# Mixture of experts on one core: the four pieces of the next expert's rows are requested in one slot, first in that slot

## Chip, cores and metric

One core of a Trainium2 chip runs the whole program. Five engines work beside each other and meet through semaphores: TensorE (PE, with its weight loads shown as PEld), VectorE (DVE), ScalarE (ACT), GpSimd (POOL) and SyncE (SP). In the part of the program that matters here, SP issues nearly all transfers, one after another. The metric is the device time of one execution in microseconds (us); lower is better.

## What is computed

Three stages follow each other: a gated linear attention, a mixture of eight experts of which each token takes one, and a dense feed-forward layer with `h * cos(h)`. The change touches the second stage:

```
for e in range(E):                       # E = 8, D = 384, F = 1024
    mask = e_idx == e
    h = np.maximum(x[mask] @ w1[e], 0.0)
    ye = h @ w2[e]
    out[mask] = gate_w[mask, None] * eom[mask, e, None] * ye
```

## The kernel before

The attention stage leaves the scaled rows of all tokens in DRAM, sorted by expert: `xs` holds 448 places (`CAP`) for each expert, a row being 384 values and the token's number (385 words). The expert stage runs from about 222 us to 505 us of the profile; the feed-forward stage after it fills the rest.

**Slots.** The expert stage is a loop over 66 slots `s` (line 314): eight slots for each expert, `s = 8e + m`, and two at the end. In slot `s` the PE multiplies one 128-wide slice of the hidden layer of expert `e` (`mm1`, nine products of 128x448, lines 622 to 625), then the second product of the slice two slots back (`mm2`, nine products, lines 201 to 203). Every product is written as three, with high and low parts of both factors: after `mm1`, ACT writes the high part `hi` (line 189) and DVE the low part `lo` (line 190). Behind these two, the list `ev[s]` of the slot is worked off in the order in which `at(s, ...)` filled it. Every engine takes its own instructions in program order, and an instruction that waits holds up all that stand behind it on its engine.

**What the list of a slot holds** (lines 283 to 307), in this order before the change:

- 24 conversions of a weight block from 64-bit numbers to 32-bit ones, for the later stage. `conv_load` issues the block (`cs`, 512 KB) three slots ahead; `conv_a` (ACT line 227, DVE lines 228 to 232) and one slot later `conv_b` (DVE lines 238 to 241) work on it; `conv_store` (line 245) writes it back.
- `W.split`: ACT rounds two quarters of an expert weight tile (`wh<-ws`, line 113), POOL subtracts for one of them and DVE for the other (`wl<-ws,wh`, line 117). `W.load` (`ws`, 384 KB, line 100) then reloads a staging buffer, four halves ahead. Its issue on SP waits until both subtractions are done.
- `trans_x(e+1, d)` in slots `8e+4`, `8e+5`, `8e+6`, for d = 0, 1, 2: the PE transposes one third of the next expert's rows, piece by piece (four transposes, line 169, one for each of the four pieces of 112 rows), into one PSUM bank. The bank has no second buffer. ACT (`yh`, line 614) and DVE (`yl`, line 615) then split it, and the transposes of the next d wait for that.
- `ids(e+1)` in slot `8e+7`: POOL copies the token numbers out of the row buffer `xe` (`id`, line 178), and SP writes them to a table in DRAM (`idtab`, line 179).
- `load_x(e+2, r)` for the pieces r = 0 to 3 (`xe<-xs`, 168 KB each, line 162), one piece in each of the slots `8e+7`, `8e+8`, `8e+9` and `8e+10`.

**What ties them.** The row buffer `xe` has one copy, so the first piece for expert e+2 can be requested only when the last transposes of expert e+1 (slot `8e+6`) and the copy of its token numbers are done. The first four transposes that read these rows stand at the end of slot `8e+12`. The rows of expert 1 are loaded ahead of the loop, all four pieces together (line 273). So six gathers, of the experts 2 to 7, lie inside the loop. "The turn to expert 3" below means the transposes in slots 20 to 22, and so on for the others.

Of the kernel before, what the change touches and what calls it, by code (L numbers as in the profile page):

```python
# [18 lines left out]
NT, DM, E, F, FF = 3072, 384, 8, 1024, 2048  # L19
# [9 lines left out]
NR = CAP // RT  # L29
# [17 lines left out]
def build(tc, A, O):  # L47
    nc = tc.nc
    sp = nc.sync
    with ExitStack() as top:  # L50
        const = top.enter_context(tc.tile_pool(name="const", bufs=1))
        dram = top.enter_context(tc.tile_pool(name="dram", bufs=1, space=DRAM))
        xs = dram.tile([XROWS, XW], F32, name="xs")
        idtab = dram.tile([NT + CAP, 1], I32, name="idtab")
        wffn = dram.tile([8, 128, PW], F32, name="wffn")

        ident = const.tile([128, 128], F32, name="ident")
        ones = const.tile([128, 128], BF16, name="ones")
        zeros = const.tile([128, 128], BF16, name="zeros")
        ctab = const.tile([128, E, GMAX], F32, name="ctab")  # L60
        acc = const.tile([128, E], BF16, name="acc")
        plast = const.tile([128, NU, NP], F32, name="plast")
        flag = const.tile([128, 1], I32, name="flag")

        with tc.manual_schedule(), ExitStack() as rows:
            c = dict(locals())
            c["W"] = W = Weights(tc, A, c, top)
            c["ya"] = top.enter_context(tc.tile_pool(name="ya", bufs=1, side="right"))
            c["xa"] = rows.enter_context(tc.tile_pool(name="xa", bufs=1, side="right"))
            attention(tc, A, c)  # L70
            W.more(top)
            moe_ffn(tc, A, O, c)
        general(tc, A, O, c)
# [50 lines left out]
def moe_ffn(tc, A, O, c):  # L124
# [8 lines left out]
    with ExitStack() as ctx:  # L133
# [15 lines left out]
        with ExitStack() as mctx:  # L149
# [130 lines left out]
            def at(s, fn, *a):  # L280
                ev.setdefault(s, []).append((fn, a))

            for i in range(24):
                t = 6 + 23 * i // 10
                at(t - 3, conv_load, i)
                at(t, conv_a, i)
                at(t + 1, conv_b, i)
                at(t + 1, conv_store, i)
# [12 lines left out]
            for e in range(E - 1):  # L301
                for d in range(KD):
                    at(8 * e + 4 + d, trans_x, e + 1, d)
                at(8 * e + 7, ids, e + 1)
                for r in range(NR):
                    if e + 2 < E:
                        at(8 * e + 7 + r, load_x, e + 2, r)


            for d in range(KD):  # L310
# [893 lines left out]
```

## Time and profile before

| | before |
|---|---|
| median of three runs | 926.71 us (918.55, 926.71, 928.77) |
| time of the profiled execution | 921.53 us |
| its span, first to last instruction | 919.7 us |
| PE busy | 832.2 us (90%) |
| DVE busy | 733.6 us (80%) |
| ACT busy, POOL busy | 386.8 us, 413.7 us |

The profile shows one execution. The time beside the span (1.8 us) lies before the first and after the last instruction. A timeline row gives start, duration, engine, line, operation and names; a bracket at its end gives how long the engine stood idle before it and what released it. A PE that is busy need not be at full speed: the granted clock of a stretch is 1.00 at 2.4 GHz and 0.50 at 1.2 GHz, and a mean between them says that both occurred. Matmuls are pipelined, so the durations of neighbouring rows overlap; pace is read from their starts.

### The profile page before, as it was taken

Reading aid. Unit: us, or ns where it says so; the run is one execution under the profiler, and the core shown is the slowest. Engines: PE = TensorE matmul, PEld = TensorE weight load, DVE = VectorE, ACT = ScalarE, POOL = GpSimd, SP = SyncE. Lnnn points to the kernel's source line nnn. Section 1 sums busy time; section 2 is a strip of 40 time slices with the busy share of each in tenths; the row PEclk is TensorE's granted clock in tenths of the full one; section 3 lists DMA queues with packets and bytes.
Section 4 is the critical chain, followed back from the end, with each engine's and each line's share of the span. In section 5 each row is a group of like instructions: output and inputs, shape, how many; then the busy total and the mean of one; then the engine's idle time right before and its main releaser. Section 6 shows DMA issues by size and latency. Waiting matters only on the chain.

```text
span 919.7 us, 14462 instructions
## 1 busy us (share of the span) xinstructions
PE 832.2 (90%) x5253; PEld 740.9 (81%) x5253; DVE 733.6 (80%) x1288; ACT 386.8 (42%) x740; POOL 413.7 (45%) x369
## 2 busy tenths in 40 slices
PE   6887677789899898898899999999999999999995
PEld 5766566677788797797799898989999999999885
DVE  6999999886797796886876887778777777787990
ACT  3674566435343343353344444333333333333440
POOL 3546575643122222221225476544644554545652
PEclk7898899798899898999989999999999999999998
DMA  9995646203675855955846200000000000000001
GB/s 185 294 308 155 172 122 174 96 28 99 163 177 174 213 130 192 222 131 199 215 145 145 36 18 1 32 4 1 35 1 0 35 1 1 35 1 1 35 1 38
DMA packets 42033, 92.26 MB, mean 100 GB/s; under 512 B 12576, under 2 KB 19872, under 8 KB 41952
## 3 DMA queue, kind: packets, MB, share of 16 engines
q1 hardware_dynamic: 38880, 81.79, 34.0%
q0 software_dynamic: 3072, 9.45, 2.8%
q8 instruction: 43, 0.70, 0.3%
q14 instruction: 38, 0.31, 0.1%
HBM read 69.93 MB, written 21.29 MB: 99 GB/s over the span
## 4 chain that ended last, share of the span: by engine, by line
PE 58%; DVE 25%; DMA 9%; issue 4%; ACT 1%; POOL 1%; SPq 1%; DVEq 0%; POOLq 0%; ACTq 0%
PE ps L622 9%; PE ps L623 9%; PE ps L625 9%; PE o L374 6%; PE o L372 6%; PE o L373 6%; DMA xe<-xs 5%; DVE r L705 4%; PE o L201 3%; PE o L202 3%; PE o L203 3%; DVE S_sb L816 3%; DVE sc L754 2%; DVE a L738 2%; DVE d L731 2%
## 5 line engine op out<-in xcount | busy, mean ns | idle before, releaser
L368 POOL TENSOR_TENSOR lo<-r,hi 128x512 fp32r<-128x512 f32 (+1 forms) x96 | 148.1, 1543 | 172.4 <-ACT hi L367 91.5
L117 POOL TENSOR_TENSOR wl<-ws,wh 128x384 fp32r<-128x384 f32 x96 | 101.3, 1055 | 220.7 <-ACT wh L113 164.8
L622 PE MATMUL ps<-yh,wh 128*128 128x512 f32 (+1 forms) x480 | 189.2, 394 | 0.2 <-ACT yh L614 0.2
L623 PE MATMUL ps<-yh,wl 128*128 128x512 f32 (+1 forms) x480 | 187.3, 390 | 0.0
L625 PE MATMUL ps<-yl,wh 128*128 128x512 f32 (+1 forms) x480 | 135.0, 390 | 0.0
L367 ACT CAST hi<-r 128x512 fp32r<-128x512 f32 (+1 forms) x96 | 56.2, 586 | 168.7 <-DVE r L362 167.8
L630 DVE TENSOR_SCALAR n<-ps 128x512 f32<-128x512 f32 x96 | 66.2, 690 | 68.6 <-PE ps L625 68.6
L374 PE MATMUL o<-wh,lo 128*128 128x384 f32 x352 | 119.0, 338 | 1.3 <-POOL lo L368 1.3
L372 PE MATMUL o<-wl,hi 128*128 128x384 f32 x352 | 118.6, 337 | 0.0
L373 PE MATMUL o<-wh,hi 128*128 128x384 f32 x352 | 118.3, 336 | 0.0
L625 PEld LDWEIGHTS ps<-yl,wh 128*128 128x128 f32 x480 | 92.9, 194 | 16.1
L622 PEld LDWEIGHTS ps<-yh,wh 128*128 128x128 f32 x480 | 93.1, 194 | 11.8 <-ACT yh L614 0.3
L623 PEld LDWEIGHTS ps<-yh,wl 128*128 128x128 f32 x480 | 92.7, 193 | 11.3
L638 ACT ACTIVATE r<-r,quarter 128x512 f32<-128x512 f32 x96 | 69.6, 724 | 73.8 <-DVE r L637 73.8
L189 ACT ACTIVATE hi<-ps 128x448 fp32r<-128x448 f32 x64 | 34.9, 545 | 101.5 <-PE ps L625 98.9
L113 ACT CAST wh<-ws 128x384 fp32r<-128x384 f32 x160 | 74.8, 508 | 4.5 <-DMA ws<-in_wmoe 4.5
L637 DVE SCALAR_TENSOR_TENSOR r<-n,r 128x512 f32<-128x512 f32 x96 | 70.1, 730 | 3.3
L201 PE MATMUL o<-hi,wh 128*128 128x448 f32 x192 | 71.9, 374 | 0.0
L202 PE MATMUL o<-hi,wl 128*128 128x448 f32 x192 | 71.5, 373 | 0.0
L203 PE MATMUL o<-lo,wh 128*128 128x448 f32 x192 | 71.2, 371 | 0.0
L373 PEld LDWEIGHTS o<-wh,hi 128*128 128x128 f32 x352 | 66.1, 188 | 4.3
L372 PEld LDWEIGHTS o<-wl,hi 128*128 128x128 f32 x352 | 66.2, 188 | 3.9
(152 smaller groups left out, 1582.2 us busy)
## 6 DMA issues: line engine op xcount, KB each, us to landing
ws<-in_wmoe SPq DMA_DIRECT2D x64, 384.0 KB, 5.9
qkf<-in_qkf SPq DMA_DIRECT2D x46, 288.0 KB, 6.4
cs<-in_wffn SPq DMA_DIRECT2D x24, 512.0 KB, 6.9
wffn<-ca SPq DMA_DIRECT2D x24, 256.0 KB, 5.2
ws<-wffn SPq DMA_DIRECT2D x16, 384.0 KB, 3.9
xs<-xe SPq DMA_DIRECT2D x7, 770.0 KB, 10.2
v<-in_v SPq DMA_DIRECT2D x24, 200.0 KB, 4.8
xe<-xs SPq DMA_DIRECT2D x28, 168.4 KB, 8.4
```

The costliest lines, as they stand in the source:

```text
L113: self.nc.scalar.copy(out=h, in_=w)
L117: (eng or self.nc.gpsimd).tensor_tensor(out=l, in0=w, in1=h.bitcast(F32), op=ALU.subtract)
L201: pe.matmul(yps[e][d], wh[:, cs], hi, start=m == 0, stop=False)
L202: pe.matmul(yps[e][d], wl[:, cs], hi, start=False, stop=False)
L203: pe.matmul(yps[e][d], wh[:, cs], lo, start=False, stop=m == FT - 1)
L368: pool.tensor_tensor(out=los, in0=r[:, cs], in1=his.bitcast(F32), op=ALU.subtract)
L372: pe.matmul(o, hi, wl[:, cs], start=m == 0, stop=False)
L373: pe.matmul(o, hi, wh[:, cs], start=False, stop=False)
L374: pe.matmul(o, lo, wh[:, cs], start=False, stop=m == NF - 1)
L622: nc.tensor.matmul(out, wh[:, ws[d]], xh[:, d, :], start=d == 0, stop=False)
L623: nc.tensor.matmul(out, wl[:, ws[d]], xh[:, d, :], start=False, stop=False)
L625: nc.tensor.matmul(out, wh[:, ws[d]], xl[:, d, :], start=False, stop=d == 2)
```

## The change

The entries for `ids` and `load_x` are put into the slots' lists first, ahead of the conversions and the weight loads, and all four pieces go into slot `8e+7`. Nothing else differs: the same instructions, buffers and sizes.

```
@@ -280,6 +280,12 @@
             def at(s, fn, *a):
                 ev.setdefault(s, []).append((fn, a))
 
+
+            for e in range(E - 1):
+                at(8 * e + 7, ids, e + 1)
+                for r in range(NR):
+                    if e + 2 < E:
+                        at(8 * e + 7, load_x, e + 2, r)
             for i in range(24):
@@ -301,10 +307,6 @@
             for e in range(E - 1):
                 for d in range(KD):
                     at(8 * e + 4 + d, trans_x, e + 1, d)
-                at(8 * e + 7, ids, e + 1)
-                for r in range(NR):
-                    if e + 2 < E:
-                        at(8 * e + 7 + r, load_x, e + 2, r)
```

SP's queue around slot 15, where the rows of expert 3 are requested, before. The row with x2 holds the weight loads of slots 14 and 15:

```order
L220 DMA cs<-in_wffn 128x512
L100 DMA ws<-in_wmoe 128x768 x2
L173 TENSOR_LOAD start
L179 REGISTER_ALU
L179 DMA idtab<-id 112x4x1
L162 DMA xe<-xs 112x385
L245 DMA wffn<-ca 128x512
L220 DMA cs<-in_wffn 128x512
L100 DMA ws<-in_wmoe 128x768
L162 DMA xe<-xs 112x385
L100 DMA ws<-in_wmoe 128x768
L162 DMA xe<-xs 112x385
```

The same place of the queue in the changed kernel:

```order
L220 DMA cs<-in_wffn 128x512
L100 DMA ws<-in_wmoe 128x768
L173 TENSOR_LOAD start
L179 REGISTER_ALU
L179 DMA idtab<-id 112x4x1
L162 DMA xe<-xs 112x385 x4
L100 DMA ws<-in_wmoe 128x768
L245 DMA wffn<-ca 128x512
L220 DMA cs<-in_wffn 128x512
L100 DMA ws<-in_wmoe 128x768 x2
```

The table write and the first piece pass the weight load of slot 15. The second piece passes, besides, a conversion's store and load and the weight load of slot 16; the third also the weight load of slot 17; the fourth, which stood just behind the rows shown, also the store and the weight load of slot 18.

On POOL, the copy of the token numbers in the same slot, before (`wl_3452` is the low part of the weight tile that slots 14 and 15 split):

```order
L117 TENSOR_TENSOR wl_3452<-ws_3301,wh_3451 128x384
L117 TENSOR_TENSOR wl_3452<-ws_3335,wh_3451 128x384
L178 COPY id_3505<-xe_3168 112x4
L117 TENSOR_TENSOR wl_3540<-ws_3375,wh_3539 128x384
```

And in the changed kernel:

```order
L117 TENSOR_TENSOR wl_3452<-ws_3302,wh_3451 128x384
L178 COPY id_3492<-xe_3156 112x4
L117 TENSOR_TENSOR wl_3452<-ws_3335,wh_3451 128x384
L117 TENSOR_TENSOR wl_3543<-ws_3375,wh_3542 128x384
```

The copy passes slot 15's subtraction and now follows that of slot 14.

## Rows read from the trace of the kernel before

**Rows 1.** Waits of the PE, 222 to 505 us: total, times, longest
```profile
PE ps L169 <- DMA xe<-xs: 22.2, 12, 2.7
```

**Rows 2.** Timeline of the PE, turn to expert 3, transposes and line 625
```profile
311.31 0.32 PE L169 MATMUL ps<-ident,xe 112*128 112x112 f32 x1 [1.47 <-DMA xe<-xs]
313.90 0.45 PE L169 MATMUL ps<-ident,xe 112*128 112x112 f32 x1 [2.28 <-DMA xe<-xs]
316.42 1.32 PE L625 MATMUL ps<-yl,wh 128*128 128x448 f32 x3
319.90 0.55 PE L169 MATMUL ps<-ident,xe 112*128 112x112 f32 x4
323.93 0.55 PE L169 MATMUL ps<-ident,xe 112*128 112x112 f32 x4
329.19 0.78 PE L625 MATMUL ps<-yl,wh 128*128 128x448 f32 x3
332.85 0.78 PE L625 MATMUL ps<-yl,wh 128*128 128x448 f32 x3
```

**Rows 3.** Windows, six turns: length; busy PE, PEld, DVE, ACT, POOL; clock; DMA share
```profile
309.30:323.93 14.63, 10.88 (x45) 9.35 (x44) 9.39 (x15) 5.09 (x12) 2.52 (x4) 0.77 0.72 233
346.26:361.49 15.23, 10.72 (x45) 9.36 (x44) 6.65 (x11) 4.35 (x9) 2.21 (x3) 0.78 0.54 183
383.68:396.62 12.94, 9.86 (x46) 8.65 (x45) 8.68 (x15) 4.40 (x10) 2.05 (x3) 0.87 0.77 250
...
sum 84.97, PE 62.75 PEld 54.69 DVE 49.21 ACT 28.94 POOL 13.65; mean PE 10.46 PEld 9.11 DVE 8.20 ACT 4.82 POOL 2.27
```

**Rows 4.** Timeline of SP's queue, slots 14 to 18: start and duration of issues
```profile
288.00 0.33 SPq L100 DMA_DIRECT2D ws<-in_wmoe  x1
...
293.85 0.33 SPq L100 DMA_DIRECT2D ws<-in_wmoe  x1
294.69 0.37 SPq L179 DMA_DIRECT2D idtab<-id  x1
295.16 0.43 SPq L162 DMA_DIRECT2D xe<-xs  x1
...
306.96 0.44 SPq L162 DMA_DIRECT2D xe<-xs  x1
```

**Rows 5.** Timeline of POOL, slots 14 and 15
```profile
286.52 1.01 POOL L117 TENSOR_TENSOR wl<-ws,wh 128x384 fp32r<-128x384 f32 x1 [3.06 <-ACT wh L113]
...
292.25 0.38 POOL L178 COPY id<-xe 112x4 f32<-112x4 f32 x1
```

**Rows 6.** Landing of row pieces: all 28 (line 162), and expert 1's four (227.4 to 229.3)
```profile
DMA to landing us min/median/max: 2.5/8.4/11.1
```
```profile
xe<-xs SPq DMA_DIRECT2D x4, 168.4 KB, 3.0
```

**Rows 7.** Windows before the turn to expert 3, columns as in rows 3
```profile
288.00:296.00 8.00, 8.00 (x41) 7.42 (x40) 6.39 (x10) 3.50 (x8) 2.51 (x3) 1.00 0.45 157
296.00:310.00 14.00, 13.84 (x69) 12.47 (x67) 12.24 (x20) 7.00 (x16) 3.04 (x3) 1.00 0.90 170
```

**Rows 8.** Timeline of DVE, turns to experts 2, 3, 4, 5 and 7
```profile
277.23 0.55 DVE L117 TENSOR_TENSOR wl<-ws,wh 128x384 fp32r<-128x384 f32 x1
...
314.96 0.62 DVE L615 TENSOR_TENSOR yl<-ps,yh 128x448 fp32r<-128x448 f32 x1
...
352.50 0.62 DVE L615 TENSOR_TENSOR yl<-ps,yh 128x448 fp32r<-128x448 f32 x1 [5.35 <-ACT yh L614]
...
388.48 0.62 DVE L615 TENSOR_TENSOR yl<-ps,yh 128x448 fp32r<-128x448 f32 x1
...
458.25 0.55 DVE L117 TENSOR_TENSOR wl<-ws,wh 128x384 fp32r<-128x384 f32 x1
```

**Rows 9.** Timeline of the PE, turn to expert 1
```profile
244.55 1.01 PE L169 MATMUL ps<-ident,xe 112*128 112x112 f32 x4 [3.59 <-DVE yl L615]
```

**Rows 10.** Windows of eight slots from turn to turn, columns as in rows 3
```profile
309.30:346.26 36.96, 33.21 (x157) 29.98 (x156) 30.97 (x50) 16.08 (x35) 9.81 (x11) 0.91 0.64 179
346.26:383.68 37.42, 32.91 (x157) 29.99 (x156) 27.51 (x43) 15.15 (x33) 8.23 (x9) 0.91 0.71 182
```

**Rows 11.** Timeline of ACT, slot 19
```profile
307.61 0.67 ACT L227 ACTIVATE ca<-cs 128x512 f32<-128x512 f32 x1 [2.95 <-DMA cs<-in_wffn]
```

## Prediction

> **What bounds the kernel now.** I first asked the waits of the PE for the expert stage (222 to 505 us). There the PE stood idle for two causes only that amount to anything: 22.2 us, in twelve waits, for the pieces of `xe` [rows 1], and once 3.59 us for a DVE subtraction [rows 9]. The reader is to see that the PE sets the pace and that the gathers alone interrupt it, twice at each of the six turns.
>
> Next I read the timeline of the PE at one turn, that to expert 3. The first two pieces had landed; the third cost 1.47 us, the fourth 2.28 us. Then the three products of line 625 took 1.32 us at 316.42 and 0.78 us at 329.19: the clock had fallen from 2.4 to 1.2 GHz after the waits [rows 2]. So the windows come third. From the first transpose of a turn to the first transpose two slots later, undisturbed, are two slots: between 319.90 and 323.93 one such slot took 4.03 us [rows 2], so two take 8.06. This turn took 14.63 us at a mean clock of 0.77; the six took 84.97 [rows 3]. The turns cost 84.97 - 6 x 8.06 = 36.6 us more than their work. Of this 22.2 us are the waits [rows 1] and the other 14.4 us, 2.4 at a turn, are matmuls at the lower clock. Outside the turns the clock is 1.00 [rows 7].
>
> Last, why the pieces are late. SP's queue is in order. For expert 3 the first piece was issued at 295.16 and the fourth at 306.96 [rows 4], 2.3 us before the transposes begin at 309.30 [rows 3], while a piece takes 8.4 us to land in the middle, 11.1 at worst [rows 6].
>
> **The change, part by part.**
>
> *The four pieces.* In the changed queue only slot 14's weight load (issued at 288.00, 0.33 us long) stands ahead of `ids`. SP arrives at 288.4 instead of 294.2, when slot 15's load ends [rows 4]. The first piece also needs the transposes of slot 14, and `ids` needs POOL's copy. POOL ends slot 14's subtraction at 286.52 + 1.01 = 287.53, and the copy takes 0.38 [rows 5], so it is done by 288. Keeping the old distance of 0.5 us from load to table write and 0.47 from that to the first piece [rows 4], the pieces go out at about 289.4, 289.9, 290.4 and 290.9. The last gains 306.96 - 290.9 = 16 us. Even the slowest landing (11.1) is then at 302, seven us ahead of need. The nearer row is that of expert 1, whose four pieces were issued together and landed in 3.0 us [rows 6]: the first gather moves into a stretch where the DMA engines are 0.45 busy, out of one where they are 0.90 [rows 7]. I take the whole 36.6 us as removed, the other turns being built alike.
>
> *What is passed.* Slot 15's `ws` load was issued at 293.85 because it waits for DVE's subtraction; SP would otherwise have stood there from 288.33 [rows 4]. Five issues of some 0.45 us fit into that wait, so on SP the move costs 0. If that wait were gone, they would cost 2.3 us a turn, on a load that is requested four slots ahead (four slots are 14.6 us, at 332.85 - 329.19 = 3.66 each [rows 2]); 0 again. On POOL the copy delays slot 15's subtraction by 0.38 us, for weights used many slots later: 0.
>
> *The DVE behind the wait.* This is the term that isn't free. The transposes of d = 1 wait until DVE has emptied the only bank, so `yl` of d = 0 has to end 4.03 us after the turn's first transpose. During the waits DVE caught up; now it has to be in time by itself. In the turn to expert 3 it worked without a break until it began `yl` at 314.96 and ended it at 315.58 [rows 8]; the PE would be there at 309.30 + 4.03 = 313.33: a new wait of 2.2 us. For expert 5: 388.48 + 0.62 = 389.10 [rows 8] against 383.68 [rows 3] + 4.03 = 387.71: 1.4 us. For expert 2 DVE's previous work ends at 277.78 [rows 8], so `yl` could end at 278.4, against a need at about 277.9: 0.5. For expert 7, 458.80 [rows 8] + 0.62 against about 459.2: 0.2. For expert 4 DVE had stood idle for 5.35 us when the bank came [rows 8], and the turn to expert 6 has the same place in the pattern of conversions: 0. Together 4.3 us. It may be less: conversion blocks were late too, ACT waiting 2.95 us for one in slot 19 [rows 11], and they now share the DMA engines with no gather there. It may be some 0.5 more where the delay reaches d = 2. I take 4.
>
> *The clock at these waits.* Rows show no lone wait between 1 and 2.2 us. Below: 0. Above: 2.4 us each, as at the gathers; the lone wait of 3.59 us at expert 1 [rows 9] did it too. I count it for the longest only: 2.4.
>
> The sum: -36.6 + 4 + 2.4 = -30 us, and 921.5 - 30 = 891.5 against the profiled execution's own time. The three runs shown stand on average 3.1 us above it (their median 5.2). Some of that may be longer gather waits, which would vanish too, so I add half: **893 us**. The likeliest case's own range is 921.5 - 36.6 = 885 to 921.5 - 36.6 + 4.8 + 3 x 2.4 = 897.
>
> **The rivals.**
>
> *DVE takes the PE's place.* For: in the eight slots from 309.30, DVE was busy 30.97 us [rows 10], and eight undisturbed slots of the PE are 5 x 3.66 + 3 x 4.03 = 30.4. Against: the next eight need only 27.51 [rows 10], so it recovers every second expert. If it doesn't recover, each turn waits as expert 3's does, 6 x 2.2 = 13 us, and half of them lose the clock, 7 us: 921.5 - 36.6 + 20 = 905.
>
> *Nothing is gained.* The pieces are issued no earlier than before because SP is held ahead of them, at `ids` or at the buffer's release, or all four land as late as the fourth does now. Then about 921. Against: POOL's copy is free by 288 and the transposes of slot 14 end beside it; and the twelve waits name only these pieces.
>
> *Slower: the burst makes ACT late.* Four pieces, 0.67 MB, stand ahead of the conversion block and weight loads of that slot. ACT takes a late block in program order, with `hi` for the PE behind it. In slot 19 it was already held 2.95 us [rows 11], without any wait of the PE for `hi`. A block has three slots, 11 us, and `hi` nearly one slot of 3.66 more, so it begins to decide when a block lands more than about 14.6 us after its issue. To end 9 us slower than now, each turn would have to lose (36.6 + 9)/6 = 7.6 us, a landing of about 22 us. The burst adds about 3 us (expert 1's landing [rows 6]), which is why I give it little. Time: 931.
> The Trainium skill ("DMA: Bandwidth & Descriptors", section on queues, rings and completion order) speaks for this mechanism: each DMA engine consumes a ring's descriptors in order, so what is issued behind the four pieces passes none of them. By that page's fit for GpSimd's path, 2.0 us plus bytes at 436 GB/s, the burst would be an estimated 3.5 us, which leaves the verdict as it is; the trace's 3.0 us decides.
>
> **How the numbers follow.** About 1% (9 us) is what a measurement of this kernel can tell from no change. Chances: the likeliest case 0.72, DVE takes the place 0.16, nothing gained 0.07, slower 0.05. The first two are both faster by over 1%: faster 0.88, same 0.07, slower 0.05. For the range I take the likeliest case's 885 to 897, widened below by the 3 us by which runs fall under the profiled one, and above to just past the DVE case at 905: 882 to 909.
>
> **What would show it.** In the changed profile: no PE wait for `xe` (22.2 us before); four issues of line 162 within 2 us, ahead of slot 8e+7's `ws`; landings near 3 to 5 us; the turns' windows near 8 to 11 us with a clock of at least 0.9; new waits of the PE for DVE's `yl` at experts 3 and 5, 4 us in all. It would be wrong if these `yl` waits came at every turn, if the clock stayed below 0.9 in the turns without a gather's wait, or if ACT's waits for `cs` grew and the PE began to wait for `hi`.

## The result and the profile after

| | before | changed |
|---|---|---|
| median | 926.61 us | 898.15 us |
| runs | 918.55 to 928.77 | 893.35 to 900.23 |
| ratio to before, 95% interval | | 0.9701 (0.9630 to 0.9772) |
| profiled execution | 921.53 us | 899.66 us |
| its span | 919.7 us | 897.9 us |

The changed kernel is 3.0% faster, 28.5 us by the medians and 21.9 by the two profiled executions. It lies in the range (882 to 909) and on the forecast side, 5 us above the forecast 893. Lines of the program after the change stand 2 higher than before: line 617 is `yl` (before 615), 627 the last product of `mm1` (before 625).

Waits in the changed kernel, 222 to 500 us (total, times, longest), and below them the landing of the pieces (from the view of line 162), which answer to [rows 1] and [rows 6]:

```profile
PE ps L169 <- DVE yl L617: 15.2, 6, 5.3
...
ACT ca L227 <- DMA cs<-in_wffn: 13.5, 5, 5.2
...
DVE cb L228 <- DMA cs<-in_wffn: 7.3, 3, 3.8
...
PE o L376 <- POOL lo L370: 0.3, 1, 0.3
```
```profile
DMA to landing us min/median/max: 8.8/11.1/11.5
```

The two lines for `cs` read before, 222 to 505 us:

```profile
ACT ca L227 <- DMA cs<-in_wffn: 7.5, 4, 2.9
...
DVE cb L228 <- DMA cs<-in_wffn: 1.4, 3, 0.6
```

No wait of the PE for `xe` is left, but the one for DVE's `yl` has grown from 3.6 us (once) to 15.2 us (six times), and ACT and DVE wait longer for the conversion blocks. The pieces land no sooner than before. The trace of the changed kernel tells a landing for six of the 28 only, the first two pieces of experts 3, 5 and 7: 8.8 to 11.5 us, where the same six took 7.7 to 11.1 before. SP's queue for expert 3, answering to [rows 4]:

```profile
286.35 0.33 SPq L100 DMA_DIRECT2D ws<-in_wmoe  x1
287.26 0.36 SPq L179 DMA_DIRECT2D idtab<-id  x1
287.72 1.84 SPq L162 DMA_DIRECT2D xe<-xs  x4
292.23 0.35 SPq L100 DMA_DIRECT2D ws<-in_wmoe  x1
295.35 0.34 SPq L245 DMA_DIRECT2D wffn<-ca  x1
295.75 0.42 SPq L220 DMA_DIRECT2D cs<-in_wffn  x1
```

All four go out within 1.84 us, 18 us ahead of the turn at 307.69 (16 to 17 us at the other five turns), so a landing of 11 us costs the PE nothing. The six turns, answering to [rows 3] (window; length; busy PE, PEld, DVE, ACT, POOL; clock; DMA share; GB/s):

```profile
273.28:285.49 12.21, 9.91 (x45) 8.76 (x44) 10.48 (x18) 4.12 (x9) 2.97 (x3) 0.86 0.70 223
307.69:317.37 9.68, 8.27 (x46) 7.39 (x45) 8.14 (x14) 4.05 (x9) 2.19 (x3) 1.00 0.70 238
339.70:352.68 12.98, 10.07 (x45) 8.59 (x44) 12.20 (x19) 5.13 (x12) 3.97 (x5) 0.87 0.57 191
375.07:384.88 9.81, 8.30 (x45) 7.38 (x44) 8.27 (x14) 4.08 (x9) 1.80 (x3) 1.00 0.75 259
407.40:417.51 10.11, 8.33 (x45) 7.38 (x44) 9.97 (x18) 4.36 (x9) 2.05 (x3) 1.00 0.63 202
439.91:447.97 8.06, 8.06 (x46) 7.47 (x45) 7.92 (x14) 4.38 (x10) 2.19 (x3) 1.00 0.68 218
sum 62.85, PE 52.94 PEld 46.96 DVE 56.98 ACT 26.11 POOL 15.18; mean PE 8.82 PEld 7.83 DVE 9.50 ACT 4.35 POOL 2.53
```

The turns fell from 84.97 to 62.85 us, by 22.1. That matches the whole difference of the two profiled executions. Against 6 x 8.06 = 48.4 us, 14.5 us are still lost. One of the turns, to expert 4, on the PE:

```profile
339.70 0.55 PE L169 MATMUL ps<-ident,xe 112*128 112x112 f32 x4
...
347.01 0.60 PE L169 MATMUL ps<-ident,xe 112*128 112x112 f32 x4 [2.91 <-DVE yl L617]
...
349.06 1.32 PE L627 MATMUL ps<-yl,wh 128*128 128x448 f32 x3
...
352.68 0.55 PE L169 MATMUL ps<-ident,xe 112*128 112x112 f32 x4
```

The transposes of d = 0 run through; those of d = 1 wait 2.91 us for `yl`, and line 627 then takes 1.32 us, as it did at 1.2 GHz before [rows 2]. What made DVE late stands on ACT and DVE some microseconds earlier:

```profile
336.57 0.67 ACT L227 ACTIVATE ca<-cs 128x512 f32<-128x512 f32 x1 [5.20 <-DMA cs<-in_wffn]
```
```profile
336.58 0.43 DVE L228 TENSOR_SCALAR cb<-cs 128x512 int32<-128x512 int32 x1 [3.79 <-DMA cs<-in_wffn]
```

Both stood for a conversion block. SP had issued it at 323.98, behind the table write, the four pieces and one store. It took 12.5 us to land (from the view of the queues, 324 to 326.5 us):

```profile
cs<-in_wffn SPq DMA_DIRECT2D x1, 512.0 KB, 12.5
```

DVE then worked all but without a break until it began `yl` at 346.34 and ended it at 346.95, 3.2 us after the PE could have used it (339.70 + 4.03 = 343.73). So the question for the runs was what slows the transfers behind the pieces: the pieces themselves, the table write, or neither, with DVE simply short of time.

### The profile page after: what moved, and what is told of

Read it like the earlier page. It is cut to its first block, busy times and chain, and to the rows that moved or that the text cites. A ratio compares the mean times of both kernels' runs of the same rounds, so it can differ in the third digit from the quotient of the medians.

```text
span 897.9 us, 14470 instructions
## 1 busy us (share of the span) xinstructions
PE 822.1 (92%) x5253; PEld 732.6 (82%) x5253; DVE 736.4 (82%) x1288; ACT 386.9 (43%) x740; POOL 413.4 (46%) x369
## 4 chain that ended last, share of the span: by engine, by line
PE 56%; DVE 28%; DMA 8%; issue 4%; ACT 1%; POOL 1%; SPq 0%; POOLq 0%; DVEq 0%; ACTq 0%
PE ps L627 9%; PE ps L625 9%; PE ps L624 9%; PE o L376 7%; PE o L374 7%; PE o L375 7%; DVE r L707 4%; DVE sc L756 3%; DMA cs<-in_wffn 2%; PE o L201 2%; PE o L202 2%; DMA ws<-in_wmoe 2%; PE o L203 2%; DVE S_sb L818 2%; DVE d L733 2%
## 5 line engine op out<-in xcount | busy, mean ns | idle before, releaser
L370 POOL TENSOR_TENSOR lo<-r,hi 128x512 fp32r<-128x512 f32 (+1 forms) x96 | 146.2, 1523 | 172.2 <-ACT hi L369 92.1
L624 PE MATMUL ps<-yh,wh 128*128 128x512 f32 (+1 forms) x480 | 186.5, 389 | 0.2 <-ACT yh L616 0.2
L625 PE MATMUL ps<-yh,wl 128*128 128x512 f32 (+1 forms) x480 | 184.9, 385 | 0.0
L627 PE MATMUL ps<-yl,wh 128*128 128x512 f32 (+1 forms) x480 | 133.0, 385 | 0.0
L624 PEld LDWEIGHTS ps<-yh,wh 128*128 128x128 f32 x480 | 91.0, 190 | 11.5 <-ACT yh L616 0.3
L625 PEld LDWEIGHTS ps<-yh,wl 128*128 128x128 f32 x480 | 91.1, 190 | 11.1
L639 DVE SCALAR_TENSOR_TENSOR r<-n,r 128x512 f32<-128x512 f32 x96 | 72.4, 755 | 3.3
## 6 DMA issues: line engine op xcount, KB each, us to landing
xe<-xs SPq DMA_DIRECT2D x28, 168.4 KB, 11.1
```

Of the source, the lines that this page charges most:

```text
L370: pool.tensor_tensor(out=los, in0=r[:, cs], in1=his.bitcast(F32), op=ALU.subtract)
L624: nc.tensor.matmul(out, wh[:, ws[d]], xh[:, d, :], start=d == 0, stop=False)
L625: nc.tensor.matmul(out, wl[:, ws[d]], xh[:, d, :], start=False, stop=False)
L627: nc.tensor.matmul(out, wh[:, ws[d]], xl[:, d, :], start=False, stop=d == 2)
```

## The experiments

Each ratio is taken against runs of the kernel before made beside it on the same chip. Their medians range from 920.34 to 926.77 us for this one kernel, so ratios are compared.

### The table write out of the slot

The write of the token numbers is split from POOL's copy, which stays first. It goes to the end of a later slot, or, for experts 3 and 5, of a slot in which the next four pieces stand first (23 and 39).

```
-                at(8 * e + 7, ids, e + 1)
+                at(8 * e + 7, ids_copy, e + 1)
...
+            for e, s in enumerate((9, 16, 23, 32, 39, 56, 57)):
+                at(s, ids_write, e + 1)
```

> The changed kernel with the table write taken out of the slot of the pieces and put at the end of a later slot (9, 16, 23, 32, 39, 56, 57); POOL's copy stays first. Theory: the table write, 448 entries of four bytes, holds the DMA rings for about 8 us; the pieces behind it land in 11 us, and so do the conversion blocks, which makes ACT and DVE late and the PE wait for yl. Then here the pieces land in 3 to 5 us, ACT's waits for cs fall from 13.5 us to under 6, the PE's waits for yl at experts 2 to 7 from 9.9 us to about 4, and the time to about 890. Rival: DVE has no time to spare, whatever the blocks do; then pieces land sooner, but the yl waits stay near 10 us and the time within 3 us of the changed kernel's 898.

Measured: 0.9591 (0.9535 to 0.9648), median 887.78 us, near the 890 of the theory. The pieces land in 3.7 us in the middle, 7.8 at most. ACT and DVE wait for no conversion block at all, though the longest of these still took 10.8 us to land. The turns read:

```profile
272.71:280.80 8.09, 8.09 (x45) 7.45 (x44) 7.83 (x14) 4.13 (x9) 2.65 (x3) 1.00 0.82 103
303.15:312.91 9.76, 8.27 (x45) 7.39 (x44) 8.21 (x14) 4.04 (x9) 1.75 (x3) 1.00 0.88 325
335.24:343.36 8.12, 8.12 (x45) 7.47 (x44) 6.54 (x11) 4.33 (x9) 2.22 (x3) 1.00 0.75 281
365.55:375.41 9.86, 8.28 (x46) 7.38 (x45) 8.31 (x14) 4.05 (x9) 1.94 (x3) 1.00 0.91 323
...
sum 52.02, PE 48.95 PEld 44.63 DVE 45.37 ACT 25.29 POOL 13.00; mean PE 8.16 PEld 7.44 DVE 7.56 ACT 4.22 POOL 2.17
```

Of the six turns only those to experts 3 and 5 still wait, 1.49 and 1.58 us, and the clock is 1.00 in all six. The turns are 10.8 us shorter than in the changed kernel, and the ratio lies 1.1% lower, about 10 us (the two intervals just overlap; the runs themselves, 884 to 888 against 893 to 900 us, do not). The write is what took back a part of the gain; but for these 3.1 us the DVE had the time. How little moves behind it shows in two windows of eight us, begun 0.4 and 1.0 us after the first piece of expert 2 was issued (first the changed kernel, where the write stands ahead of the pieces, then this one; columns as above):

```profile
255.00:263.00 8.00, 8.00 (x41) 7.19 (x40) 7.51 (x17) 3.00 (x6) 1.32 (x2) 1.00 0.92 58
```
```profile
254.00:262.00 8.00, 8.00 (x41) 7.23 (x40) 7.57 (x16) 2.99 (x6) 1.84 (x2) 1.00 0.81 262
```

The DMA engines are counted busy in both, at 58 GB/s behind the write and 262 GB/s without it. Windows begun likewise at the other five gathers give 67 to 165 GB/s behind the write and 276 to 322 without it.

### The write directly behind the pieces

From the kernel just shown, the write goes back into slot 8e+7, behind the four `load_x`.

```
-            for e, s in enumerate((9, 16, 23, 32, 39, 56, 57)):
-                at(s, ids_write, e + 1)
...
+                at(8 * e + 7, ids_write, e + 1)
```

> The changed kernel with the table write directly behind the four pieces instead of ahead of them; the conversion block and weight loads of the slot still stand behind it. The pieces land in about 3 us instead of 11. If late pieces were what is left, the time falls to about 888 as in a_late. Theory: the pieces had slack; what hurts is the late conversion block behind the write, so ACT still waits over 9 us for cs, the PE 8 to 12 us for yl at experts 2 to 7, and the time stays at 895 to 900.

Measured: 0.9742 (0.9671 to 0.9813), median 899.03 us, as the theory had it. The pieces landed in 3.8 us in the middle, and it gained nothing over the changed kernel. ACT still waited 15.7 us for blocks and DVE 7.3, and of the 14.2 us that the PE waited for `yl` 10.6 lay at experts 2 to 7 (222 to 500 us):

```profile
ACT ca L230 <- DMA cs<-in_wffn: 15.7, 5, 5.1
...
PE ps L169 <- DVE yl L621: 14.2, 6, 3.6
...
DVE cb L231 <- DMA cs<-in_wffn: 7.3, 3, 3.7
```

So late pieces are harmless where they are issued 16 to 18 us ahead; the late conversion blocks behind the write are not. Nor was it SP: in the changed kernel SP's later issues waited 12.7 us for the table write's landing (222 to 480 us), here for none, and the time is no better.

### Two banks for the transposes

```
-            ps_h = mctx.enter_context(tc.tile_pool(name="ps_h", bufs=4, space=PSUM, **reuse))
-            ps_t = mctx.enter_context(tc.tile_pool(name="ps_t", bufs=1, space=PSUM, **reuse))
+            ps_h = mctx.enter_context(tc.tile_pool(name="ps_h", bufs=3, space=PSUM, **reuse))
+            ps_t = mctx.enter_context(tc.tile_pool(name="ps_t", bufs=2, space=PSUM, **reuse))
```

> The changed kernel with two PSUM banks for the transposes and three instead of four for the first product. The transposes of the next third then need not wait for yl of the one before. If the new waits for yl are what the change left on the path, the PE's waits for yl (15.2 us with the turn to expert 1) go to under 2 us, the clock in the turns to 1.00, and the time to about 880. If DVE is the bound as a whole, the wait moves to the matmuls of the next expert or to the second product, and the time stays above 893.

Measured: 0.9655 (0.9594 to 0.9716), median 891.23 us, between the two forecasts. The transposes' wait for `yl` fell to 0.3 us, but others came up: 4.9 us at line 627, which reads `yl`, 1.8 at line 203 for `lo`, and 1.8 for a guard's small product in slot 8. ACT waited 25.9 us for blocks, 13.5 in the changed kernel. A second bank moves part of the wait past the transposes; it does not bring the blocks sooner.

> Both: the table write later and two PSUM banks for the transposes. Theory: the two act on one wait, so that together they give little more than the second bank alone: 876 to 882. Rival, separate losses: each gives its own gain, 872 or less.

Measured, with the write moved as well: 0.9548 (0.9488 to 0.9607), median 882.73 us. That is just above the theory's 876 to 882, and against the write alone (0.9591) the difference is inside the intervals. Of the six turns of its profiled execution none waits any more. Its only wait for `yl` at transposes, 1.1 us, is at the turn to expert 1.

### The two halves of the change

Order alone: each piece, and the write, first in its slot, but in four slots.

```
-                        at(8 * e + 7, load_x, e + 2, r)
+                        at(8 * e + 7 + r, load_x, e + 2, r)
```

> Half of the change: the table write and each piece stand first in their slot, but the pieces stay spread over slots 8e+7 to 8e+10. The fourth piece then goes out where slot 8e+9 ends on SP, one slot (about 3 us) sooner than before. Theory: the gain came mainly from the three slots that merging saves; the PE's waits for xe fall from 22 to 8 to 14 us and the time to 905 to 914. Rival, that the place ahead of the slot's other transfers is what counts: waits under 4 us, time under 902.

Measured: 0.9625 (0.9556 to 0.9695), median 887.71 us. The theory missed by some 20 us and the rival holds: 1.9 us of waits for `xe`, and a time at least as short as that of the whole change. The pieces of expert 3 in SP's queue:

```profile
282.06 0.43 SPq L162 DMA_DIRECT2D xe<-xs  x1
286.58 0.35 SPq L100 DMA_DIRECT2D ws<-in_wmoe  x1
286.98 0.42 SPq L162 DMA_DIRECT2D xe<-xs  x1
...
291.09 0.73 SPq L162 DMA_DIRECT2D xe<-xs  x1
...
297.00 0.85 SPq L162 DMA_DIRECT2D xe<-xs  x1
```

The fourth piece goes out 5.2 us ahead of its turn (302.23), where it had 2.3 before, and this turn waits for no piece. Over the six turns the fourth pieces went out 5.1 to 7.1 us ahead instead of 1.7 to 3.6, about 3 us sooner. They landed in 3.3 to 7.4 us instead of 6.1 to 8.7, about 1 us less, though the middle of all pieces is 8.3 (8.4 before). So it was mostly the time of issue that did it, and by a small margin: 1.9 us of waits are left at two other turns. The waits for `yl` at experts 2 to 7 are 1.8 us instead of 9.9. With one piece and not four between the write and the slot's block, ACT waits 10.4 us for blocks and DVE 2.5, against 13.5 and 7.3.

Merging alone: four pieces in slot 8e+7, at the old place behind the slot's other transfers (the line of the kernel before, with `8 * e + 7` for `8 * e + 7 + r`).

> The other half: all four pieces in slot 8e+7, at the old place behind the slot's other transfers. They go out some 5 to 6 us later than in the changed kernel, still 12 us ahead of need, with a landing of about 11 us. Theory: hardly any wait for xe is left (under 3 us), and the time is within 5 us of the changed kernel's 898. Rival: the place at the head matters; waits for xe above 8 us and a time above 906.

Measured: 0.9799 (0.9725 to 0.9872), median 903.43 us, just outside the 5 us of the theory and below the rival's 906: no wait for `xe`, but 17.1 us for `yl`, 12.5 of them at experts 2, 3, 5 and 7, and 14.4 us of ACT's for blocks. Either half by itself removes the waits for the gather, or all but 1.9 us of them. Order gives hardly anything back, and merging pays with late blocks. The whole change (0.9701) lies between the two, but its interval overlaps both; only the two halves are apart beyond their intervals.

### The write alone, in the kernel before

The same split, with the same new slots for the write, in the kernel before; all else stays in place.

> The kernel before with the table write alone put later, in the same slots as in a_late; the four pieces stay in four slots, behind the slot's other work. Theory of the table write: the first pieces land in 3 to 5 us instead of 9, the later ones somewhat sooner, and the PE's waits for xe fall from 22.2 us to under 12; time near 908. Rival, that only the time of issue counts: the last piece is issued as late as before, 2 us ahead of need, the waits stay at 18 us or more, and the time above 918.

Measured: 1.0015 (0.9987 to 1.0043), median 926.43 us, and the waits for `xe` rose to 27.8 us. The place was badly chosen: at five of the six turns the write stood between the pieces, for expert 2 at 269.76, ahead of the fourth at 271.54, whose wait grew from 1.10 to 5.52 us. (At the turn to expert 7, where it did not, the waits fell from 4.0 to 2.4 us.) It shows the cost of the write to what follows it, but doesn't answer the question that it was made for. So it was put behind the fourth piece (slots 10, 18, 26, 34, 42, 50, 58):

> The kernel before, with only the table write moved behind the fourth piece (end of slot 8e+10); b_late had put it between the pieces. Nothing of the write is then ahead of the pieces of its own gather. Theory: the pieces' landing falls to 4 to 5 us in the middle, the waits for xe from 22 us to under 8, the time to about 905. Rival, issue is too late whatever the landing: waits above 15 us and a time above 915.

Measured: 0.9859 (0.9782 to 0.9937), median 910.13 us, with both forecasts half right. The pieces landed in 3.5 us in the middle (the first ones, with no write ahead of them any more, in 3.2 to 4.7 us instead of 7.7 to 9.9) and the third no longer made the PE wait, but the fourth did at all six turns, 19.4 us, of which 5.07 and 6.55 us at experts 4 and 6. Issue was too late for it whatever the middle landing. At those two turns it took 7.2 and 8.7 us to land. There a conversion block had gone out between the third piece and the fourth, at 335.33 and 407.03, and at the other turns none had; whether that is the cause was not tested.

### Spreading, with the rest

> order_only (pieces first in four slots) with the table write moved behind the fourth piece's slot, at the end of slots 10, 19, 28, 35, 42, 51 and 58. If the write still costs where the pieces are spread, ACT's waits for cs fall below 6 us (10.4 in order_only), the last xe wait (1.9 us) goes, and the time falls to about 884. If spreading had already hidden it: within 2 us of order_only's 887.7.

Measured: 0.9603 (0.9545 to 0.9661), median 889.7 us. Blocks cost ACT 0.4 us and there was no wait for `xe`, yet the ratio is that of order alone within the interval: where the pieces are spread, most of the write's cost is hidden. The wait at the turn to expert 1 stayed (5.22 us).

> order_only with two PSUM banks for the transposes and three for the first product. The waits of the PE for yl (6.4 us, 4.6 of them at the turn to expert 1, with a lower clock behind that one) go: about 880. If DVE is bound there as a whole, the wait moves to the products that read yl and lo, and the time stays above 885.

Measured: 0.9575 (0.9520 to 0.9631), median 889.57 us. The time was forecast at about 880 and is 10 us above; what came instead is a wait for `xe` again, 7.4 us at four turns. The fourth piece was issued as far ahead as in order alone, within 0.3 us at five turns and 0.8 less at expert 2, but at the four turns that waited it took 6.3 to 8.8 us to land instead of 5.7 to 7.4. Why it did is open.

> Everything that has helped: pieces first in four slots, table write later, two banks for the transposes. The PE without any wait in six turns needs 6 x 8.06 us there, so about 877 to 880; not below 875, since the turn to expert 1 and the DVE work ahead of expert 2 remain.

Measured: 0.9537 (0.9489 to 0.9585), median 885.91 us, against 926.77 of the kernel before beside it and 6 us above the forecast. All six turns run without a wait. By the ratio this is the best version, together with the changed kernel with late write and two banks (0.9548), from which it cannot be told apart.

## Why the prediction was right, and where it was off

- **What bounds the kernel: right.** The gathers' waits were on the PE's path, and all 22.2 us of them went.
- **Issue: right.** For expert 3 the first piece was forecast 1.4 us behind slot 14's weight load (289.4 against 288.00) and the four issues over 1.5 us; measured 1.37 us behind it (287.72 against 286.35) and 1.4 us, with SP paying nothing for it: the slot's `ws` load still went out when DVE's subtraction released it.
- **Landing: wrong.** I took expert 1's 3.0 us [rows 6]; the six landings that the trace tells are 8.8 to 11.5. That row has no table write ahead of it, the loop's pieces do. I moved the write along and counted its issue, not what it does to the transfers behind it. In the trace of before the first piece behind it had already taken 7.7 to 9.9 us, which I read as a crowded stretch. Late pieces cost nothing, since the lead was 16 to 18 us.
- **Waits for `yl`: right in kind, too small.** Forecast 4.3 us from late DVE work (2.2 at expert 3, 1.4 at 5, 0.7 at 2 and 7 together), taken as 4; measured 9.9, as 2.30, 1.41, 2.91, 1.51 and 1.78 at experts 2 to 6. (The sixth wait, 5.33 us at expert 1, stands ahead of all that the change moves; it was 3.59 before, and 3.5 to 5.2 in the other runs with one bank.) Without late blocks, with the write moved, it is 1.49 and 1.58 at experts 3 and 5 alone: there the working of that term holds in place and roughly in size. The step that failed is "conversion blocks ... now share the DMA engines with no gather there": they queued behind the write and four pieces instead. This is the mechanism of the third rival, which I had priced at nothing below a landing of 14.6 us, because I followed only `hi` to the PE. At 12.5 us it already reached the PE, through DVE and `yl`. Of the last sign of being wrong that I named, one half came true, ACT's waits for `cs` (7.5 to 13.5 us), and the other, a wait of the PE for `hi`, did not.
- **The clock: mis-sized.** Forecast once, 2.4 us; it fell twice, at experts 2 and 4, for 12.21 - 8.06 - 2.30 = 1.9 and 12.98 - 8.06 - 2.91 = 2.0 us. The 2.4 was a mean over turns that differ: before, the turn to expert 5 (clock 0.87, waits of 0.90 and 2.18 us) lost 12.94 - 8.06 - 3.08 = 1.8 us to the clock, that to expert 3 (0.77) 14.63 - 8.06 - 3.75 = 2.8.
- **The sum.** Forecast 36.6 - 6.4 = 30 us against the profiled execution, measured 22: the turns lose 14.5 us instead of 6.4. By the medians the gain was 28.5. That the time came within 5 us of the forecast was in part luck: before, the profiled execution is 5 us below the median, and in the changed kernel it is 1.5 above; between these two executions the gain was 8 us smaller than forecast.
- **The rivals.** DVE did take a part, by late blocks and not by a lack of time. "Nothing gained" is out. The write at the head of the burst cost about 10 us, near a third of the 36.6 that the change could give and far from the 46 that a loss needed. The four pieces themselves did not: with the write moved they stand ahead of the block as before, and ACT waits for none.

## What to carry to other kernels

In an in-order queue, where a request stands can matter more than how many go together: first in its slot instead of last was nearly enough for each piece here (0.9625). Bunching the four cost time only with the table write in the same slot: with the write elsewhere, bunched (0.9591) and spread (0.9603) cannot be told apart. Before a group is moved to the head of a queue, every transfer in it has to be followed to its landing, the small ones too, and what then stands behind it has to be followed to its users on every engine.

## What the runs showed of the hardware

A table write of 1.8 KB (448 entries of four bytes) took 6.6 to 10.2 us to land in the kernel before, 9.0 in the middle, and up to 12.1 in the other runs. In the eight us behind it its queue moved 58 to 165 GB/s, and 262 to 322 without it. The Trainium skill ("DMA: Bandwidth & Descriptors", specifications) gives 512 bytes as the smallest transfer at line rate; these entries are far below it, and the runs agree in direction.

Wherever the traces tell the landings on SP's queue, 147 of them in the kernel before, they come in the order of issue: nothing issued behind the write or the pieces was seen to pass them.

The clock was not lowered by each wait. In the turns with waits of 1.41 to 1.78 us the changed kernel's clock is 1.00, with 2.30 and 2.91 us it is 0.86 and 0.87, a mean of both levels. Two turns of the kernel with the write behind the pieces lie closer: with 1.81 us (first) and 2.08 us (second).

```profile
342.42:352.60 10.18, 8.37 (x45) 7.38 (x44) 10.04 (x18) 4.34 (x9) 2.41 (x3) 1.00 0.64 204
374.99:386.94 11.95, 9.87 (x46) 8.70 (x44) 8.86 (x15) 4.64 (x11) 2.38 (x3) 0.86 0.65 224
```

The wait of 2.08 us therefore cost 11.95 - 8.06 = 3.9 us in all, that of 1.81 us 2.1 us. No fixed limit and no fixed price follows from this. In the run with the pieces spread and two banks, the turn to expert 2 kept a clock of 1.00 through a wait of 2.15 us:

```profile
270.34:280.84 10.50, 8.35 (x45) 7.46 (x44) 10.15 (x19) 5.27 (x11) 2.63 (x3) 1.00 0.79 240
```

And 2.89 us at expert 6, with the write behind the pieces, cost 14.20 - 8.06 - 2.89 = 3.3 us beyond the wait (clock 0.76), where 2.91 us in the changed kernel cost 2.0.
